# A fused sliding-window attention and feed-forward kernel: half-width PV matmuls in two batches, a reordered start, a split last tile

## The chip, the core and the metric

The kernel runs on one core of one Trainium2 chip. TensorE is called PE (its weight loads PEld), VectorE DVE, ScalarE ACT, GpSimd POOL and SyncE SP, as in the profile. The metric is the time of one launch on the device, in microseconds (us). Each engine works through its own instructions in program order, and semaphores order the engines among each other. DMAs are issued from the queues of SP and POOL, and after the change from ACT's as well.

## The reference

Eight batches of eight heads attend over 576 positions with head dimension 64. A query sees only itself and the 63 keys before it. The heads are joined to 512 columns, and a multiplicative feed-forward network follows.

```
def _attn_ref(q, k, v):              # 8 x 8 x 576 x 64, float32
    scores = scale * np.matmul(q, k.transpose(0, 1, 3, 2))
    rel = pos[:, None] - pos[None, :]
    scores = np.where((rel >= 0) & (rel < 64), scores, -1e9)
    attn = softmax(scores)
    return np.matmul(attn, v)

def _moe_ref(x, w1, w2, w3, w_out):  # x is 4608 x 512
    a = x @ w1                       # 512 -> 1024
    b = x @ w2
    h = a * b @ w3                   # 1024 -> 1024
    return h @ w_out                 # 1024 -> 512
```

## The kernel before, in words

**The weights are folded.** Since nothing nonlinear stands between them, w3 and w_out are multiplied once into one matrix `wc_sb`. `fold_t(fc)` transposes one of eight row blocks of w3 on PE (L446) and copies it out of PSUM on DVE (L448); `fold_mm(fc)` multiplies it with w_out on PE (L454, eight matmuls of 512 columns) and casts the result into `wc_sb` (L455). Two row blocks of w3 arrive with one DMA, `load_w3` (L439); w_out arrives whole with `load_wo` (L433). Both are cast to fp16 on the way, and so are v (`load_v`, L233) and w1 and w2 (`load_w12`, L429); all of these are issued from POOL.

**Attention** takes a batch in six units d of 192 queries by four heads (two head pairs jj, with heads a = 0 and 1 of each). q and k of a batch come from SP's queue (`load_qk`, L206), two DMAs each, one for each half hh of the heads. They are cast to fp16 (L221 in thirds for batch 0, L214 in halves later) and transposed on PE (L253) into PSUM tiles that DVE or ACT copies out (L257). For a unit, `scores(d)` makes the transposed scores (PE, L278), their exponential (ACT, L282) and the window mask with two or four selects (POOL, L290 and L292). `values(d)` is the product PV on PE (L311): eight matmuls, whose 128 weight columns are one head's 64 columns of v and 64 columns of ones, so that the output and the softmax sum of a head come out together, on the two halves of the partitions, for a = 0 and a = 1 the other way round. Then ACT takes the logarithm of the sums in two pieces of 64 partitions (L320, L321) and the exponential of its negative (L323), and DVE multiplies in two pieces of 64 partitions (L326, L327) into `xT`, the transposed input of the network. The tile `o_ps` of this product has one buffer, so the next unit's product waits for the last multiplication. The logarithms are also kept (`lnsum`, L332) for a range check at the end.

**The network** takes groups of 512 tokens: `ffn_ab(g, fc)` (PE L395; ACT copy L400; DVE product L401) and `ffn_o(g, t)` (PE L408; DVE copy L410), with the result stored from SP (L417).

**The order** is written out by hand for the first two batches: a start with dummy matmuls `keep_busy(n)` (L479) on PE between the waits, then batch 0's six values interleaved with the fold, then batch 1's with group 0 of the network. From there on a planner interleaves the units of batches 2 to 7 with the groups 1 to 8. At the start, POOL clears the ones columns of both v buffers (`ones_of`, L488), and then issues w_out, the first piece of w3, three blocks of v, three pieces of w3 and two more blocks of v. PSUM has eight banks: one for `tp`, two each for `s_ps` and `o_ps` (one tile each), and three tiles `f_ps` of one bank. `spare` hands out the two banks of an `s_ps` or `o_ps` tile for transposes.

Of the kernel before, what the change touches and what calls it, by code (L numbers as in the profile page):

```python
# [8 lines left out]
FP32 = mybir.dt.float32  # L9
FP16 = mybir.dt.float16  # L10
I32 = mybir.dt.int32
ALU = mybir.AluOpType
AF = mybir.ActivationFunctionType
PSUM = bass.MemoryType.PSUM

P = 128
# [128 lines left out]
def kernel(  # L145
# [11 lines left out]
    nc = tc.nc  # L157
    B, H, S, D = q.shape
    N = B * S
    DM = H * D  # L160
    DF = moe_w3.shape[0]
    scale = 1.0 / (D ** 0.5)
    NJ = H // 2
    TP, TI = 32, 18
    GT = 512
    NG = N // GT
    RING = 4 * S
    NU = 12 * B
    ND = 6 * B

    keep = ctx.enter_context(tc.tile_pool(name="keep", bufs=1))
    ident16 = keep.tile([P, P], FP16)
# [15 lines left out]
    dve_cp = nc.vector.tensor_copy  # L188
# [8 lines left out]

    raws, k16s, q16s = {}, {}, {}

    def load_qk(b, which, gate=None):  # L200
        src = k if which == "k" else q
        t = sb.tile([P, 2, TI * D], FP32, name="stage", bufs=4)
        if gate is not None:
            gate(t[:, 0, 0:1], 0.0)
        for hh in range(2):
            nc.sync.dma_start(out=t[:, hh], in_=src[b, hh:H:2].rearrange("j (p r) d -> p j (r d)", r=TI))  # L206
        raws[which, b] = t

    def cast_qk(b, which, hh, cp):
# [6 lines left out]
    def cast_third(b, which, c, cp):  # L216
        t = raws[which, b]
        if c == 0:
            (k16s if which == "k" else q16s)[b] = sb.tile([P, TI, P], FP16, name=which + "16", bufs=1)
        t16 = (k16s if which == "k" else q16s)[b]  # L220
        cp(t16[:, 6 * c:6 * c + 6].rearrange("p i (hh d) -> p hh i d", hh=2),  # L221
           t[:, :, 6 * c * D:6 * c * D + 6 * D].rearrange("p hh (i d) -> p hh i d", d=D))
# [4 lines left out]
    def load_v(b, *blocks):  # L227

        vh = v_heads(b)
        for c in blocks:  # L230
            lo = D if c == 4 else 0
            s0 = VBLK[c] + lo
            nc.gpsimd.dma_start(out=vh[lo:P, c], in_=v[b, :, s0:s0 + P - lo, :].rearrange("h s d -> s h d"))  # L233
# [10 lines left out]
    def transposes(b, which, *cs, into=None, cps=None):  # L244

        t16, dst = (k16s, kTs) if which == "k" else (q16s, qTs)
        if cs[0] == 0:
            dst[b] = sb.tile([P, NJ, S], FP16, name=which + "T")
        if into is None:
            into = [ps_t.tile([P, 6, P], FP16, name="tp")]  # L250
        for c, tp in zip(cs, into):
            for i in range(6):
                nc.tensor.transpose(tp[:, i, :], t16[b][:, 6 * c + i, :], ident16)  # L253
        if cps is None:
            cps = [dve_cp if which == "k" or c != 1 else act_cp for c in cs]
        for c, tp, cp in zip(cs, into, cps):
            cp(dst[b].rearrange("q j (p i) -> q j p i", i=TI)[:, :, :, 6 * c:6 * c + 6],  # L257
               tp.rearrange("q i (p j) -> q j p i", p=TP))
# [37 lines left out]
    def values(d):  # L296
        b, r = divmod(d, 6)
        si, jp = divmod(r, 2)
        j0 = 2 * jp
        v16 = v16s[b % 2]  # L300
        pt = probs.pop(d)
        seg = SEGS[si]
        q_base = seg[0][1]
        o_ps = ps_v.tile([P, 2, 512], FP32, name="o_ps")
        for jj in range(2):
            first = True
            for a in range(2):
                c0 = 0
                for bi, (k0, q0, n, _) in enumerate(seg):
                    o0 = a * 192 + q0 - q_base  # L310
                    nc.tensor.matmul(o_ps[:, jj, o0:o0 + n],  # L311
                                     v16[:, si * 2 + bi, j0 + jj, a * D:a * D + P],
                                     pt[:, a, jj, c0:c0 + n],
                                     start=first, stop=(bi == 1), skip_group_check=True)
                    first = False
                    c0 += n
        if jp == 0:
            lns[b, si] = sb.tile([P, NJ, 192], FP32, name="ln_s", bufs=4)
        y = lns[b, si][:, j0:j0 + 2]
        nc.scalar.activation(y[0:D], o_ps[D:P, :, 0:192], AF.Ln)  # L320
        nc.scalar.activation(y[D:P], o_ps[0:D, :, 192:384], AF.Ln)  # L321
        r = sb.tile([P, 2, 192], FP32, name="r")
        nc.scalar.activation(r, y, AF.Exp, scale=-1.0)  # L323
        x0 = (b * S + q_base) % RING
        xs = xT[:, j0:j0 + 2, x0:x0 + 192]
        nc.vector.tensor_tensor(xs[0:D], o_ps[0:D, :, 0:192], r[0:D], ALU.mult)  # L326
        nc.vector.tensor_tensor(xs[D:P], o_ps[D:P, :, 192:384], r[D:P], ALU.mult)  # L327

# [74 lines left out]

    def ffn_o(g, t):
        ab = abs_[g]
        o_ps = ps_f.tile([P, DM], FP32, name="f_ps")
        for fc in range(8):
            nc.tensor.matmul(o_ps, ab[:, fc, t * P:t * P + P], wc_sb[:, fc, :], start=(fc == 0), stop=(fc == 7))  # L408
        o_sb = sb.tile([P, DM], FP32, name="t2k", bufs=4)
        dve_cp(o_sb, o_ps)  # L410
        r0 = g * GT + t * P
        stores.append((r0, o_sb))

    def store():
        while stores:
            r0, o_sb = stores.pop()
            nc.sync.dma_start(out=out[r0:r0 + P, :], in_=o_sb)  # L417

    wo16 = sb.tile([P, 8, DM], FP16, name="ab", bufs=3)
    w3a = sb.tile([P, 8, DM], FP16, name="ab", bufs=3)  # L420
# [14 lines left out]
    def load_w3(n):  # L435
        fc = 2 * n
        dst = w3a[:, 2 * fc:2 * fc + 4, :].rearrange("p (f a) n -> p f (a n)", f=2) if n < 2 else \
            xT[:, fc - 4:fc - 2, 2 * S:2 * S + DF]
        nc.gpsimd.dma_start(out=dst, in_=moe_w3[fc * P:fc * P + 2 * P].rearrange("(f p) n -> p f n", p=P))  # L439

    def fold_t(fc):

        w3 = w3_rows(fc).rearrange("p a (e n) -> p (a e) n", n=P)
        tp = ps_f.tile([P, 8, P], FP16, name="f_ps")
        for ec in range(8):
            nc.tensor.transpose(tp[:, ec, :], w3[:, ec, :], ident16)  # L446
        w3T = sb.tile([P, 8, P], FP16, name="t2k", bufs=4)
        dve_cp(w3T, tp)  # L448
        return w3T

    def fold_mm(fc, w3T, cp):
        o_ps = ps_f.tile([P, DM], FP32, name="f_ps")
        for ec in range(8):
            nc.tensor.matmul(o_ps, w3T[:, ec, :], wo16[:, ec, :], start=(ec == 0), stop=(ec == 7))  # L454
        cp(wc_sb[:, fc, :], o_ps)  # L455
# [19 lines left out]
    def keep_busy(n):  # L475

        d = ps_t.tile([P, P], FP32, name="tp")
        for _ in range(n):
            nc.tensor.matmul(d, ident16, ident16, start=True, stop=True)  # L479


    load_qk(0, "k")
    load_qk(0, "q")
    nc.scalar.preload_act_table_set("natural_log_exp_and_others")
    make_identity(nc, ident16)

    def ones_of(i):
        nc.gpsimd.memset(v16s[i].rearrange("p c j (a e) -> p (c j a) e", a=2)[:, :, D:2 * D], 1.0)  # L488

    ones_of(0)  # L490
    ones_of(1)
    load_wo()
    load_w3(0)
    load_v(0, 0, 2, 3)
    for n in range(1, 4):
        load_w3(n)
    load_v(0, 4, 5)

    w3Ts = {}

    def fold_step(fc):
        if fc + 1 < 8:
            w3Ts[fc + 1] = fold_t(fc + 1)
        fold_mm(fc, w3Ts.pop(fc), act_cp if fc % 4 == 3 else dve_cp)

    def spare(pool, name):

        t = pool.tile([P, 2, 1024], FP16, name=name)
        return [t[:, i, 0:768].rearrange("p (i n) -> p i n", i=6) for i in range(2)]

    keep_busy(75)
    tps = spare(ps_s, "s_ps") + spare(ps_v, "o_ps")
    for c in range(3):
        cast_third(0, "k", c, act_cp if c == 1 else dve_cp)
    transposes(0, "k", 0, 1, 2, into=tps, cps=[dve_cp, act_cp, dve_cp])
    keep_busy(10)
    for c in range(3):
        cast_third(0, "q", c, act_cp if c == 1 else dve_cp)
    tps = [tps[3], ps_t.tile([P, 6, P], FP16, name="tp"), spare(ps_s, "s_ps")[0]]
    transposes(0, "q", 0, 1, 2, into=tps, cps=[act_cp, dve_cp, act_cp])  # L520
    keep_busy(15)
    scores(0)
    keep_busy(10)
    scores(1)
    keep_busy(30)
    for i in range(2):
        load_w12(i, 0)
    w3Ts[0] = fold_t(0)
    fold_step(0)
    fold_mm(1, w3Ts.pop(1), dve_cp)  # L530
    copy_v(0, 1)
    for d in range(5):
# [21 lines left out]
    cast_qk(1, "q", 1, act_cp)  # L554
    values(5)
    fold_step(7)
    transposes(1, "k", 0, 1, into=spare(ps_s, "s_ps"))
    transposes(1, "k", 2)
    for n in range(3):
        keep_sums(n)  # L560
    load_v(1, 5)
# [1 line left out]
    load_qk(2, "q")  # L563
    load_v(2, 0, 2, 3)
    ffn_ab(0, 0)
    transposes(1, "q", 0, 1, into=spare(ps_s, "s_ps"))
    transposes(1, "q", 2)
    copy_v(1, 1)


# [6 lines left out]
    for d in range(6, 11):  # L577
# [10 lines left out]
        else:  # L588
            which, hh = [("k", 0), ("k", 1), ("q", 0), ("q", 1)][d - 7]
            cast_qk(2, which, hh, pool_cp)  # L590
    transposes(2, "k", 0, 1, into=spare(ps_s, "s_ps"))
    values(11)
    transposes(2, "k", 2)
    for hh in range(2):
        cast_qk(3, "k", hh, pool_cp)
    ffn_o(0, 3)
    store()
    transposes(2, "q", 0, 1, into=spare(ps_s, "s_ps"))
    transposes(2, "q", 2)
    copy_v(2, 1)  # L600
    copy_v(2, 4)
    load_qk(3, "q")
# [68 lines left out]
```

## Time and profile before

| | us |
|---|---|
| median of 9 runs | 296.5 |
| lowest and highest of them | 296.13 and 297.53 |
| the profiled execution's own time | 297.87 |
| its span, first to last instruction | 295.9 |
| PE busy | 276.3 (93%) |
| POOL, DVE and ACT busy | 180.7, 185.5 and 168.4 |
| mean granted TensorE clock | 0.991 of full |

The profile shows one execution. A timeline row gives the start, the duration, the engine, the line, the operation, the tiles (out<-in), the form and the count of the instructions merged in it; in brackets stand the idle time before it and what ended that. A row of the chain of waits gives start, duration and what was under way; "issue" is time for which the profile shows no wait. A row of the windows gives the stretch, its length, the busy time of PE, PEld, DVE, ACT and POOL with instruction counts, the granted clock of TensorE, the mean busy share of the DMA engines (over 1 where packets overlap) and GB/s.

### The profile page before, as it was taken

Reading aid. Unit: us, or ns where it says so; the run is one execution under the profiler, and the core shown is the slowest. Engines: PE = TensorE matmul, PEld = TensorE weight load, DVE = VectorE, ACT = ScalarE, POOL = GpSimd, SP = SyncE. Lnnn points to the kernel's source line nnn. Section 1 sums busy time; section 2 is a strip of 40 time slices with the busy share of each in tenths; the row PEclk is TensorE's granted clock in tenths of the full one; section 3 lists DMA queues with packets and bytes.
Section 4 is the critical chain, followed back from the end, with each engine's and each line's share of the span. In section 5 each row is a group of like instructions: output and inputs, shape, how many; then the busy total and the mean of one; then the engine's idle time right before and its main releaser. Section 6 shows DMA issues by size and latency. Waiting matters only on the chain.

```text
span 295.9 us, 5925 instructions
## 1 busy us (share of the span) xinstructions
PE 276.3 (93%) x2254; PEld 154.5 (52%) x2254; DVE 185.5 (63%) x289; ACT 168.4 (57%) x281; POOL 180.7 (61%) x214
## 2 busy tenths in 40 slices
PE   7768998899889999999999999999999999999992
PEld 7654545444545555555555787555555444444440
DVE  0713688655796666778868766677868655554541
ACT  2421875586448638775686565497668866642300
POOL 8735897378839956597769453786595443402200
PEclk9998999999999999999999999999999999999998
DMA  6999999983267928295909380970095021012012
GB/s 235 211 181 201 262 275 200 364 134 52 73 209 309 80 93 287 88 65 134 336 19 112 120 309 2 116 112 1 3 160 66 0 74 72 0 38 108 0 59 92
DMA packets 51665, 38.85 MB, mean 131 GB/s; under 512 B 38784, under 2 KB 41856, under 8 KB 51632
## 3 DMA queue, kind: packets, MB, share of 16 engines
q0 software_dynamic: 41744, 9.96, 36.2%
q1 hardware_dynamic: 9888, 28.46, 26.5%
q8 instruction: 19, 0.31, 0.4%
q14 instruction: 14, 0.11, 0.1%
HBM read 38.80 MB, written 9.44 MB: 163 GB/s over the span
## 4 chain that ended last, share of the span: by engine, by line
PE 76%; DVE 6%; ACT 5%; DMA 4%; issue 3%; POOL 3%; POOLq 0%; DVEq 0%; ACTq 0%
PE f_ps L395 38%; PE f_ps L408 19%; PE o_ps L311 7%; PE tp L253 5%; DMA ab<-in_moe_w_dram 4%; PE s_ps L278 4%; PE f_ps L454 2%; DVE xT L327 2%; ACT ln_s L321 2%; ACT r L323 2%; POOL v L488 2%; DVE kT L257 1%; DVE xT L326 1%; ACT ln_s L320 1%; ACT pt L282 1%
## 5 line engine op out<-in xcount | busy, mean ns | idle before, releaser
L395 PE MATMUL f_ps<-xT,w_sb 128*128 128x512 f16 (+1 forms) x640 | 134.1, 358 | 0.0
L290 POOL TENSOR_SCALAR_AFFINE_SELECT pt<-pt 128x512 f16<-128x512 f16 (+1 forms) x64 | 52.1, 814 | 70.5 <-ACT pt L282 70.4
L395 PEld LDWEIGHTS <-w_sb 128*128 128x128 f16 x640 | 59.7, 98 | 50.8 <-issue 0.5
L408 PE MATMUL f_ps<-wc_sb,ab 128*128 128x512 f16 x288 | 67.1, 379 | 0.1
L401 DVE TENSOR_TENSOR ab<-f_ps,a_sb 128x512 f16<-128x512 f32 x72 | 49.8, 692 | 18.4 <-PE f_ps L395 15.7
L326 DVE TENSOR_TENSOR xT<-o_ps,r 64x384 f16<-64x384 f32 x48 | 26.4, 549 | 53.9 <-ACT r L323 52.4
L282 ACT ACTIVATE pt<-s_ps 128x1024 f16<-128x1024 f32 (+1 forms) x48 | 45.5, 949 | 18.2 <-PE s_ps L278 16.7
L400 ACT COPY a_sb<-f_ps 128x512 f32<-128x512 f32 x72 | 41.7, 579 | 24.8 <-PE f_ps L395 23.9
L292 POOL TENSOR_SCALAR_AFFINE_SELECT pt<-pt 128x512 f16<-128x512 f16 (+1 forms) x64 | 52.4, 819 | 4.4
L320 ACT ACTIVATE ln_s<-o_ps 64x384 f32<-64x384 f32 x48 | 23.4, 487 | 53.9 <-PE o_ps L311 53.8
L408 PEld LDWEIGHTS <-ab 128*128 128x128 f16 x288 | 26.9, 98 | 28.8 <-DVE ab L401 0.6
L233 POOL DMA_DIRECT2D v<-in_v_dram x40 | 33.9, 855 | 6.1 <-DMA ab<-in_moe_w_out_dram 4.3
L311 PE MATMUL o_ps<-pt,v 128*128 128x128 f16 (+1 forms) x384 | 27.9, 215 | 5.8 <-DVE xT L327 4.0
L311 PEld LDWEIGHTS <-v 128*128 128x128 f16 x384 | 23.6, 98 | 18.1 <-issue 4.7
L410 DVE COPY t2k<-f_ps 128x512 f32<-128x512 f32 x36 | 24.7, 690 | 11.6 <-PE f_ps L408 11.1
L327 DVE TENSOR_TENSOR xT<-o_ps,r 64x384 f16<-64x384 f32 x48 | 26.9, 561 | 0.7
L323 ACT ACTIVATE r<-ln_s 128x384 f32<-128x384 f32 x48 | 25.1, 522 | 1.5
L321 ACT ACTIVATE ln_s<-o_ps 64x384 f32<-64x384 f32 x48 | 23.1, 482 | 0.5
L278 PEld LDWEIGHTS <-kT 64*128 64x128 f16 x384 | 10.5, 94 | 16.4 <-issue 14.8
L278 PE MATMUL s_ps<-qT,kT 64*128 64x128 f16 (+1 forms) x384 | 18.2, 214 | 0.3 <-ACT pt L282 0.2
L454 PE MATMUL f_ps<-ab,t2k 128*128 128x512 f16 x64 | 16.6, 409 | 0.4 <-DVE t2k L448 0.3
L257 DVE COPY kT<-tp 128x768 f16<-128x768 f16 x17 | 16.2, 952 | 0.1
(59 smaller groups left out, 182.7 us busy)
## 6 DMA issues: line engine op xcount, KB each, us to landing
stage<-in_k_dram SPq DMA_DIRECT2D x16, 576.0 KB
stage<-in_q_dram SPq DMA_DIRECT2D x16, 576.0 KB
out_dram<-t2k SPq DMA_DIRECT2D x36, 256.0 KB
v<-in_v_dram POOLq DMA_DIRECT2D x32, 128.0 KB, 4.8
w_sb<-in_moe_w_dram POOLq DMA_DIRECT2D x4, 512.0 KB, 9.1
ab<-in_moe_w_out_dram POOLq DMA_DIRECT2D x1, 1024.0 KB, 10.6
ab<-in_moe_w_dram POOLq DMA_DIRECT2D x2, 512.0 KB, 12.8
xT<-in_moe_w_dram POOLq DMA_DIRECT2D x2, 512.0 KB, 16.4
```

What stands on the lines that cost most here:

```text
L233: nc.gpsimd.dma_start(out=vh[lo:P, c], in_=v[b, :, s0:s0 + P - lo, :].rearrange("h s d -> s h d"))
L278: nc.tensor.matmul(s_ps[:, a, jj, c0:c0 + n], kT[half, j, k0:k0 + P], qT[half, j, q0:q0 + n], start=True, stop=True, skip_group_check=True)
L282: nc.scalar.activation(pt[:, :, :, 0:w], s_ps[:, :, :, 0:w], AF.Exp, bias=-SHIFT, scale=scale)
L290: nc.gpsimd.affine_select(out=sl, in_=sl, pattern=pat, compare_op=ALU.is_ge, fill=0.0, base=off, channel_multiplier=-1)
L292: nc.gpsimd.affine_select(out=sl, in_=sl, pattern=[[-s, m] for s, m in pat], compare_op=ALU.is_ge, fill=0.0, base=63 - off, channel_multip ...
L311: nc.tensor.matmul(o_ps[:, jj, o0:o0 + n], v16[:, si * 2 + bi, j0 + jj, a * D:a * D + P], pt[:, a, jj, c0:c0 + n], start=first, stop=(bi = ...
L323: nc.scalar.activation(r, y, AF.Exp, scale=-1.0)
L327: nc.vector.tensor_tensor(xs[D:P], o_ps[D:P, :, 192:384], r[D:P], ALU.mult)
L395: nc.tensor.matmul(d[:, f * n + c0:f * n + c1], w[:, dc, (fc + f) * P:(fc + f + 1) * P], xT[:, dc, xc:xc + c1 - c0], start=first, stop=(dc ...
L400: act_cp(a_sb[:, 0:nf * n], a_ps[:, 0:nf * n])
L401: nc.vector.tensor_tensor(ab[:, fc:fc + nf, lo:hi], b_ps[:, 0:nf * n].rearrange("p (f n) -> p f n", f=nf), a_sb[:, 0:nf * n].rearrange("p ...
L408: nc.tensor.matmul(o_ps, ab[:, fc, t * P:t * P + P], wc_sb[:, fc, :], start=(fc == 0), stop=(fc == 7))
```

## The change

1. **PV in batches 0 and 1** (`SHORT = 2`). The eight matmuls with 128 weight columns become sixteen with 64: for every head, v alone and the ones alone. Head a writes the partitions a*64 to a*64+63, v into bank e = 0 of `o_ps` and the ones into bank e = 1. So both heads' outputs lie in one bank over all partitions and both sums in the other, and one logarithm, one exponential and one multiplication of 128 partitions do the unit. The other batches keep the old form.
2. **First loads.** `load_qk` takes a second queue; for batch 0 the half hh = 1 of k and of q is issued from ACT.
3. **POOL's order at the start.** The first piece of w3 goes ahead of w_out, and `ones_of(1)` goes behind the last block of v.
4. **PE's order at the start.** `fold_t(0)` and `fold_t(1)` move between and behind the first two scores; the dummy matmuls are 6, 4 and 45 in place of 15, 10 and 30. The casts and copies of q are dealt out differently between ACT and DVE.
5. **Banks of the transposes.** `spare` goes; `bank` hands out one bank of a tile, and `three()` takes one of `o_ps`, one of `tp` and one of `s_ps`. k of batch 0 uses the three `f_ps` tiles.
6. **The last output tile** is computed in two halves of 256 columns, one copied by ACT and stored from ACT's queue, the other copied by DVE and stored from SP's. `store()` takes from the front of its list.

```diff
-    def load_qk(b, which, gate=None):
+    def load_qk(b, which, gate=None, other=None):
...
-            nc.sync.dma_start(out=t[:, hh], in_=...)
+            (other if hh and other else nc.sync).dma_start(out=t[:, hh], in_=...)
...
     def values(d):
...
+        if b < SHORT:
+            for jj in range(2):
+                c0 = 0
+                for bi, (k0, q0, n, _) in enumerate(seg):
+                    o0 = jj * 192 + q0 - q_base
+                    for e in range(2):
+                        for a in range(2):
+                            nc.tensor.matmul(o_ps[a * D:a * D + D, e, o0:o0 + n],
+                                             v16[:, si * 2 + bi, j0 + jj, (2 * a + e) * D:(2 * a + e) * D + D],
+                                             pt[:, a, jj, c0:c0 + n],
+                                             start=(jj == 0 and bi == 0), stop=(bi == 1), skip_group_check=True)
+                    c0 += n
+            o, total = (o_ps[:, e, 0:384].rearrange("p (j n) -> p j n", j=2) for e in range(2))
+            nc.scalar.activation(y, total, AF.Ln)
+            nc.scalar.activation(r, y, AF.Exp, scale=-1.0)
+            nc.vector.tensor_tensor(xs, o, r, ALU.mult)
+            return
...
     def ffn_o(g, t):
...
+        halves = [(0, DM, dve_cp)] if (g, t) != (NG - 1, 3) else [(0, 256, act_cp), (256, DM, dve_cp)]
+        for c0, c1, cp in halves:
+            o_ps = ps_f.tile([P, DM], FP32, name="f_ps")
+            for fc in range(8):
+                nc.tensor.matmul(o_ps[:, 0:c1 - c0], ab[:, fc, t * P:t * P + P], wc_sb[:, fc, c0:c1], ...)
+            cp(o_sb[:, c0:c1], o_ps[:, 0:c1 - c0])
+            stores.append((r0, c0, c1, o_sb))
 
     def store():
         while stores:
-            r0, o_sb = stores.pop()
-            nc.sync.dma_start(out=out[r0:r0 + P, :], in_=o_sb)
+            r0, c0, c1, o_sb = stores.pop(0)
+            queue = nc.scalar if c1 - c0 < DM and c0 == 0 else nc.sync
+            queue.dma_start(out=out[r0:r0 + P, c0:c1], in_=o_sb[:, c0:c1])
...
-    load_qk(0, "k")
-    load_qk(0, "q")
+    load_qk(0, "k", other=nc.scalar)
+    load_qk(0, "q", other=nc.scalar)
...
     ones_of(0)
-    ones_of(1)
+    load_w3(0)
     load_wo()
-    load_w3(0)
     load_v(0, 0, 2, 3)
     for n in range(1, 4):
         load_w3(n)
     load_v(0, 4, 5)
+    ones_of(1)
...
+    def bank(pool, name):
+        t = pool.tile([P, 2, 1024] if name != "f_ps" else [P, 1, 1024], FP16, name=name)
+        return t[:, 0, 0:768].rearrange("p (i n) -> p i n", i=6)
+    def tp_bank():
+        return ps_t.tile([P, 6, P], FP16, name="tp")
+    def three():
+        return [bank(ps_v, "o_ps"), tp_bank(), bank(ps_s, "s_ps")]
 
     keep_busy(75)
...
-    transposes(0, "k", 0, 1, 2, into=tps, cps=[dve_cp, act_cp, dve_cp])
+    transposes(0, "k", 0, 1, 2, into=[bank(ps_f, "f_ps") for _ in range(3)], cps=[dve_cp, act_cp, dve_cp])
     keep_busy(10)
     for c in range(3):
-        cast_third(0, "q", c, act_cp if c == 1 else dve_cp)
+        cast_third(0, "q", c, dve_cp if c == 2 else act_cp)
...
-    keep_busy(15)
+    transposes(0, "q", 0, 1, 2, into=three(), cps=[act_cp, dve_cp, act_cp])
+    keep_busy(6)
     scores(0)
-    keep_busy(10)
+    keep_busy(4)
+    w3Ts[0] = fold_t(0)
     scores(1)
-    keep_busy(30)
+    w3Ts[1] = fold_t(1)
+    keep_busy(45)
     for i in range(2):
         load_w12(i, 0)
-    w3Ts[0] = fold_t(0)
-    fold_step(0)
+    fold_mm(0, w3Ts.pop(0), dve_cp)
     fold_mm(1, w3Ts.pop(1), dve_cp)
...
-    transposes(1, "k", 0, 1, into=spare(ps_s, "s_ps"))
-    transposes(1, "k", 2)
+    transposes(1, "k", 0, 1, 2, into=three())
...
-    transposes(2, "k", 0, 1, into=spare(ps_s, "s_ps"))
+    transposes(2, "k", 0, 1, into=[bank(ps_s, "s_ps"), tp_bank()])
     values(11)
     transposes(2, "k", 2)
...
-    transposes(2, "q", 0, 1, into=spare(ps_s, "s_ps"))
-    transposes(2, "q", 2)
+    transposes(2, "q", 0, 1, 2, into=three())
```

q of batch 1 is changed as k of batch 1 is.

## The prediction

> **What bounds the kernel now.** I read the windows first, to see where PE is not full, then the timeline of those stretches, then the chain of waits, then the last rows. Two windows:
>
> ```profile
> 20.00:40.00 20.00, 17.94 (x163) 9.87 (x161) 10.75 (x20) 9.14 (x16) 15.41 (x20) 0.91 1.29 246
> ...
> 100.00:120.00 20.00, 20.00 (x161) 10.50 (x160) 13.88 (x24) 11.75 (x20) 13.59 (x17) 1.00 0.65 181
> ```
>
> From about 91 us to 290 us PE is busy all the time, in code that the change leaves alone but for its last tile. A shift won before 91 us therefore reaches the end whole, and nothing else does but the tail. Before 91 us PE waits, and at 20 to 40 us it also has a clock of only 0.91. The timeline tells why:
>
> ```profile
> 16.03 1.85 PE L479 MATMUL tp<-ident 128*128 128x128 f16 x30
> ...
> 17.46 0.70 POOL L233 DMA_DIRECT2D v<-in_v_dram  x1 [4.25 <-DMA ab<-in_moe_w_out_dram]
> ...
> 19.75 1.07 PE L446 MATMUL f_ps<-ident,ab 128*128 128x128 f16 x16 [1.87 <-DMA ab<-in_moe_w_dram]
> ...
> 21.15 5.20 PE L454 MATMUL f_ps<-ab,t2k 128*128 128x512 f16 x16 [0.34 <-DVE t2k L448]
> ```
>
> PE idles from 17.88 to 19.75 for the first piece of w3. The clock then drops (0.58 in the window 20.4 to 23.8), and the sixteen fold matmuls take 5.20 us; at the 0.216 us apart that L454 shows later they would take 3.46. The first values, behind them, run at 27.78. From there the chain of waits repeats every 3.4 to 3.5 us:
>
> ```profile
> 37.97 0.62 PE o_ps L311 x8
> 38.64 0.47 issue
> 39.11 0.49 ACT ln_s L321
> 39.62 0.53 ACT r L323
> 40.22 0.53 issue
> 40.74 0.57 DVE xT L327
> 41.36 0.64 PE o_ps L311 x8
> ```
>
> The reader should see a ring: product, two logarithms (the first hides under "issue"), exponential, two multiplications, next product. In such a period PE issues 3.05 us of work and stands 0.43 us. In batch 1 the same wait costs PE, by its waits from 59 to 91 us:
>
> ```profile
> PE o_ps L311 <- DVE xT L327: 1.9, 3, 0.7
> PE tp L253 <- DVE kT L257: 1.2, 1, 1.2
> ```
>
> The end:
>
> ```profile
> 290.05 0.69 DVE L410 COPY t2k<-f_ps 128x512 f32<-128x512 f32 x1 [1.03 <-PE f_ps L408]
> ```
>
> SP issues the last store at 290.77, the trace's semaphore records have it landed at 293.93, and 1.97 us of closing steps follow.
>
> [...] the last L311 and the first L278 matmul, which uses half the rows, start 0.152 us apart where the spacing is 0.055, so a switch costs 0.10. [...] This trace has only row halves: L278 starts in pairs 3 ns apart, a pair every 0.055 us. [...] the four first loads land at 5.56, 6.97, 8.57 and 10.01, 590 KB every 1.4 to 1.6 us, some 410 GB/s.
>
> **The change, part by part.** The times are of the profiled execution.
>
> *PV, on PE.* 12 units have 16 weight loads and matmuls in place of 8. If the a = 0 and a = 1 matmuls pair as L278's do, eight pairs stream as many columns as eight matmuls did: 0.44 us for 128 columns each. The mode switch on entering adds 0.10, uneven pairing and slower weight loads say 0.05: **+0.15 a unit**, which I take. It can't be below 0. Without pairing it is 16 x 0.055 + 0.10 - 0.44 = +0.54; with a whole weight load (98 ns in L311's row) exposed each time 16 x 0.098 + 0.10 - 0.44 = +1.23. The range takes the first two; the last is a rival.
>
> *PV, the ring.* One logarithm (0.49) and one multiplication (0.56) go. L320 takes 0.487 on 64 partitions and L323 0.522 on 128 with as many elements a partition, so the remaining ones keep their length. The ring falls from 3.48 to about 2.6 and no longer binds; PE's 3.05 + 0.15 does, or POOL.
>
> *POOL at the start.* `ones_of(1)` takes 2.66 us (L488) and leaves the front, so every DMA of this queue is issued 2.66 us sooner, the first w3 piece at 4.05 in place of 7.72. It shares the engines with q until about 9.5; I count w3 landed at 12 and w_out (5.1 us of data at the 205 GB/s that the packets reach later) at 18.0, where w_out and w3 together took until 19.70. Behind w_out stand three blocks of v and the other w3 pieces as before; they move with it, the second piece to about 22.2 (24.76 before), just ahead of `fold_t(2)`. ACT issues two loads (about 0.6 each) ahead of its table load (1.28): done by 3.5, hidden under the wait for k. k's earlier landing gains little, because `keep_busy(75)` holds PE until 8.46.
>
> *PE at the start.* Separate banks let ACT copy kT without waiting for DVE (2.43 before), ACT takes two thirds of q's casts as its copies end (q still lands at 10.0, so little moves), and nine dummies fewer let `scores(0)` go at 13.9 (14.50 before). `fold_t(0)`, `scores(1)` and `fold_t(1)` fill PE to 16.2, 45 dummies of 0.056 to 18.7. Then w_out is there, the clock is full, and `fold_mm(0)` and `(1)` end at 22.3 (before 26.4). With the cast (0.69) and the two copies of v (0.6) the first values come at 23.75. POOL: the last v block waits for w_out (18.0), takes 0.9, then comes the moved memset to 21.55 and four selects (2.1) to 23.7, level with PE. **-4.0 here**; if w_out lands 1.5 us later, everything moves with it and -2.5 remains.
>
> *Batch 0.* POOL's selects and DMA issues now follow without a gap and end unit 5 at 40.3 (PE's values(5) at 44.86 before). What is late next is the DMA of batch 1's q: issued 12.3 us before its landing at 44.62, and ACT's cast of it began at 44.65, ahead of unit 5's logarithm. Issued 4.1 sooner, beside w1 and w2 that are now still moving, I have it land at 40.8; cast 1.15, logarithm at 42.1, where 45.82 was: -3.7. The transposes of k now wait for unit 5's multiplication, since they use its bank: **-3.6 on leaving batch 0**.
>
> *Banks later.* The 0.4 us that PE waits at 50.5 for s_ps goes: **-0.4**. At 77 to 83 us the stall of 1.2 only moves: the third kT transpose now waits for the copy of the second out of tp, where the third of q did. 0, within 0.3.
>
> *Batch 1.* 1.9 us of waits go, 6 x 0.15 of PE come, and POOL (selects 2.25 and a cast 1.14 a unit, 3.4) lets only half of the rest through: **-0.5**.
>
> *Tail.* The last copy is 256 columns, about 0.42 in place of 0.69, and the last DMA half as long (0.3); two more semaphores cost 0.1: **-0.4**. The half matmuls (L395's 256-column ones, 0.109 apart) cost nothing more. ACT is idle there. The order of `store()` changes nothing, as one tile at a time is pending.
>
> Sum: -3.6 - 0.4 + 0 - 0.5 - 0.4 = **-4.9**. On 297.87 that is 293.0; the median of the runs shown is 1.37 lower, so **291.6**.
>
> **The rivals.**
> 1. *PV in single file, weight loads hidden* (+0.54 a unit). For: no column pair in the trace. Against: the row pairs. Batch 1 turns from -0.5 to +1.3, batch 0 loses about 0.5: -2.6, **293.9**.
> 2. *DMA binds the start.* w_out lands at 19.5, as its slow beginning (102 and 127 KB a us at 9 to 11 us) may recur: -1.5 less, **293.1**; with q of batch 1 late too, 294.5.
> 3. *Nothing binds behind the start*: q in time, POOL faster because DVE does less: -7, **289.5**.
> 4. *Slower: exposed weight loads.* PE becomes the bound of both batches: of some 8.2 us to win with a free PV, PE's growth eats 11 units' worth, so the sign turns at +0.75 a unit, a mean spacing of 69 ns for the sixteen matmuls. At 98 ns (+1.23) the kernel loses 5.3: **301.8**. [...]
> 5. *The change is not what it says*: the pairs would not be next to each other. They are in PE's program, 104 matmuls more.
>
> **How the numbers follow.** A measurement here can tell about 0.2% (0.6 us) from no change. Forecast (289.9 to 292.9) 0.52, rival 1 0.14, rival 2 0.13, rival 3 0.08, rival 4 0.10, and 0.03 for cancelling effects between. Slower: rival 4 and a little of 1 and 2, 0.12; same 0.05; faster 0.83. The range 289.4 to 295.3 takes in rivals 1 to 3 and leaves rival 4 out.
>
> **What would show it.** After: no wait of PE for w3 near 20 us and clock 1.00 there; L454's first sixteen in 3.5 us; first values near 23.8; sixteen PV matmuls in pairs, 0.5 us a unit; one logarithm and one multiplication; ACT's cast of q waiting for its DMA near 41; PE full from about 87; last landing 3 us before the end. PV spaced over 69 ns, or first values after 26 us, would make it wrong.

## The result, and the profile after

The changed kernel takes **292.22 us** (median of 10 runs, 290.9 to 293.27) where the kernel before takes 296.44 (31 runs). The ratio is 0.9849, with a 95% interval from 0.9832 to 0.9865. The forecast was 291.6 with a range of 289.4 to 295.3. The total was right, but the experiments show that its parts were not: the start was put too high, the gain from the short PV too low, and the banks had the wrong sign.

The profiled execution after took 291.12 us, with a span of 289.2. That is 6.7 less than the span before, more than the medians' 4.2, because the profiled execution before lay 1.4 above its median and this one lies 1.1 below its own.

First the two windows that were shown of before, now of after:

```profile
20.00:40.00 20.00, 18.42 (x211) 10.49 (x210) 13.62 (x22) 10.35 (x16) 19.44 (x24) 1.00 1.22 257
100.00:120.00 20.00, 20.00 (x162) 10.39 (x160) 14.52 (x23) 12.74 (x23) 11.62 (x16) 1.00 0.48 171
```

From 20 to 40 us the clock is full (1.00, before 0.91), and POOL has become the busiest engine, with 19.44 us of 20 (15.41 before). At 100 us PE is as full as before.

The timeline of the start:

```profile
16.20 2.68 PE L503 MATMUL tp<-ident 128*128 128x128 f16 x45
...
18.71 3.62 PE L478 MATMUL f_ps<-ab,t2k 128*128 128x512 f16 x16
18.99 2.68 POOL L512 MEMSET v<- 128x3072 f16 x1
...
23.31 0.62 PE L470 MATMUL f_ps<-ident,ab 128*128 128x128 f16 x8 [0.98 <-DMA ab<-in_moe_w_dram]
23.86 0.58 PE L320 MATMUL o_ps<-pt,v 128*64 128x128 f16 x16
```

The wait for w3's first piece is gone, the fold's sixteen matmuls take 3.62 us in place of 5.20, and the first PV runs at 23.86 in place of 27.78. A new wait of 0.98 us for w3's second piece stands just ahead of it. The end of batch 0:

```profile
41.10 0.64 PE L320 MATMUL o_ps<-pt,v 128*64 128x128 f16 x16 [1.18 <-POOL pt L293]
41.49 1.15 ACT L215 CAST q<-stage 128x1152 f16<-128x1152 f32 x1 [1.72 <-DMA stage<-in_q_dram]
...
42.55 0.48 ACT L326 ACTIVATE ln_s<-o_ps 128x384 f32<-128x384 f32 x1
...
44.24 0.50 PE L254 MATMUL o_ps<-ident,k 128*128 128x128 f16 x6 [0.67 <-ACT wc_sb L479]
```

PE waits for POOL's select; ACT's only logarithm of unit 5 stands behind the cast of batch 1's q, which waited for its DMA; and the transposes of k come after that. In batch 1 one stall of PE remains:

```profile
74.14 0.50 PE L254 MATMUL tp<-ident,k 128*128 128x128 f16 x6 [1.27 <-DVE kT L258]
```

The shares of the chain of waits, which no longer has much of DVE and ACT (6% and 5% before):

```profile
PE 77%; DMA 11%; POOL 4%; DVE 2%; ACT 1%; issue 1%; SPq 1%; POOLq 0%; ACTq 0%
```

### The profile page after: what moved, and what is told of

Same layout as the page of the kernel before. It is cut to its first block, busy times and chain, and to the rows that moved or that the text cites. A ratio compares the mean times of both kernels' runs of the same rounds, so it can differ in the third digit from the quotient of the medians.

```text
span 289.2 us, 6101 instructions
## 1 busy us (share of the span) xinstructions
PE 274.6 (95%) x2358; PEld 155.3 (54%) x2358; DVE 179.7 (62%) x276; ACT 164.2 (57%) x271; POOL 180.9 (63%) x214
## 4 chain that ended last, share of the span: by engine, by line
PE 77%; DMA 11%; POOL 4%; DVE 2%; ACT 1%; issue 1%; SPq 1%; POOLq 0%; ACTq 0%
PE f_ps L414 39%; PE f_ps L432 22%; DMA stage<-in_q_dram 6%; DMA ab<-in_moe_w_dram 5%; PE o_ps L336 5%; PE tp L254 5%; PE s_ps L279 4%; PE o_ps L320 1%; POOL v L234 1%; POOL v L512 1%; SPq L207 1%; POOL pt L293 1%; POOL pt L291 1%; DVE t2k L434 1%; PE f_ps L478 1%
## 5 line engine op out<-in xcount | busy, mean ns | idle before, releaser
L432 PE MATMUL f_ps<-wc_sb,ab 128*128 128x512 f16 (+1 forms) x296 | 67.0, 373 | 0.1
L345 DVE TENSOR_TENSOR xT<-o_ps,r 64x384 f16<-64x384 f32 x36 | 19.8, 550 | 39.6 <-ACT r L344 39.6
L432 PEld LDWEIGHTS <-ab 128*128 128x128 f16 x296 | 27.6, 98 | 27.9 <-issue 0.3
L342 ACT ACTIVATE ln_s<-o_ps 64x384 f32<-64x384 f32 x36 | 17.6, 488 | 32.6 <-PE o_ps L336 32.6
L434 DVE COPY t2k<-f_ps 128x512 f32<-128x512 f32 (+1 forms) x36 | 24.5, 683 | 13.2 <-PE f_ps L432 12.7
L336 PEld LDWEIGHTS <-v 128*128 128x128 f16 x288 | 18.1, 98 | 8.7 <-ACT pt L283 0.8
L336 PE MATMUL o_ps<-pt,v 128*128 128x128 f16 (+1 forms) x288 | 20.7, 215 | 0.4 <-POOL pt L293 0.4
L346 DVE TENSOR_TENSOR xT<-o_ps,r 64x384 f16<-64x384 f32 x36 | 20.2, 560 | 0.5
L344 ACT ACTIVATE r<-ln_s 128x384 f32<-128x384 f32 x36 | 18.9, 525 | 1.2
L343 ACT ACTIVATE ln_s<-o_ps 64x384 f32<-64x384 f32 x36 | 17.4, 483 | 0.4
L258 DVE COPY kT<-tp 128x768 f16<-128x768 f16 x18 | 17.1, 952 | 0.2
L326 ACT ACTIVATE ln_s<-o_ps 128x384 f32<-128x384 f32 x12 | 5.9, 491 | 18.5 <-PE o_ps L320 18.5
```

The costliest lines, as they stand in the source:

```text
L336: nc.tensor.matmul(o_ps[:, jj, o0:o0 + n], v16[:, si * 2 + bi, j0 + jj, a * D:a * D + P], pt[:, a, jj, c0:c0 + n], start=first, stop=(bi = ...
L432: nc.tensor.matmul(o_ps[:, 0:c1 - c0], ab[:, fc, t * P:t * P + P], wc_sb[:, fc, c0:c1], start=(fc == 0), stop=(fc == 7))
L434: cp(o_sb[:, c0:c1], o_ps[:, 0:c1 - c0])
```

## The experiments

Each kernel ran in five rounds beside the kernel before, so each has a ratio to it. The difference of a kernel to the changed kernel is that of the two ratios times 296.4 us; its interval is the root of the sum of squares of the two half-widths. The table puts five profiles side by side (times in us from the span's start; for before, after and three experiments that are told below).

| | before | e1: change without short PV | e2: short PV alone | after | f1: five edits on top |
|---|---|---|---|---|---|
| first PV of batch 0 goes through | 27.78 | 23.80 | 26.32 | 23.86 | 21.59 |
| PV of unit 5 | 44.86 | 41.32 | 42.43 | 41.10 | 39.67 |
| scores(6) | 55.17 | 54.94 | 52.23 | 51.52 | 49.47 |
| scores(12) | 84.81 | 86.68 | 78.57 | 79.03 | 75.82 |
| span | 295.9 | 297.0 | 289.7 | 289.2 | 286.0 |
| ratio of times to before | 1 | 1.002 | 0.9819 | 0.9849 | 0.975 |

### PV: taken out, alone, in one batch, in all

**e1_old_pv** is the change with the old PV.

```diff
-    SHORT = 2
+    SHORT = 0
```

> The changed kernel with SHORT = 0: the new start, banks and tail, but PV as before in all batches. Theory (the short PV gives batch 0 only one logarithm and one multiplication behind its last unit, about 1.0 us, because POOL and q's landing hold the rest, and batch 1 about 2.1): first values still near 23.9, 292.2 + 3.1 = 295.3 us. Rival (the shorter ring carries batch 0 too, 0.4 us a unit): 297.3 us. Rival (the start carries nearly all, as the prediction's sum has it with 0.5 for batch 1): 293.5 us.

Measured: **297.81 us**, ratio 1.002 (1.000 to 1.0041), which is 297.0 against the 296.4 of before. The rival with the full ring gain (297.3) is the nearest; the other two expectations were too low. Without the short PV the other five parts bring nothing, or lose; the short PV is worth 5.1 ± 0.8 us in the change. The table says where the start's lead goes: 4.0 us at the first PV, 3.5 at unit 5, 0.2 at scores(6), and a loss of 1.9 at scores(12). The timeline of e1 shows it:

```profile
46.00 0.73 PE L254 MATMUL o_ps<-ident,k 128*128 128x128 f16 x6 [2.14 <-DVE xT L346]
...
47.80 2.75 PE L414 MATMUL f_ps<-xT,w_sb 128*128 128x512 f16 x8
...
80.12 0.72 PE L254 MATMUL tp<-ident,k 128*128 128x128 f16 x6 [1.75 <-DVE kT L258]
80.63 3.39 PE L432 MATMUL f_ps<-wc_sb,ab 128*128 128x512 f16 x8
```

k's transposes now need the bank of `o_ps`, and wait 2.14 us for the second multiplication of the old PV. (Before, they ran in `s_ps` while that multiplication was still due.) At the second place the third block of k waits for the copy out of `tp`. After both waits TensorE's clock is down: eight matmuls of 512 columns take 2.75 and 3.39 us where they take 1.89 elsewhere, and the mean granted clock is 0.89 in the windows 45 to 60 and 75 to 90 us, 1.00 in the one between. So the long PV and the new banks hurt each other. No kernel ran with the old PV, the new start and the old banks, so how much of the start's lead the old PV alone would have left is not known.

**e2_only_pv** is the kernel before with the new block of `values` and nothing else.

```diff
+        if b < SHORT:      # SHORT = 2, sixteen matmuls, one logarithm, one exponential, one multiplication
...
+            return
```

> The kernel before with the short PV in batches 0 and 1 and nothing else. Theory: values(0) stays at 27.8, q of batch 1 still lands near 44.6 and holds the last logarithm of batch 0, so batch 0 gives about 1.0 us and batch 1 about 2.1: 296.4 - 3.1 = 293.3 us. Rival (behind an unchanged start q's landing eats all of batch 0, and batch 1 is worth the predicted 0.5): 295.7 us.

Measured: **291.39 us**, ratio 0.9819 (0.9794 to 0.9844), better than every expectation. One part of the change gives at least what the whole gives (the whole is 0.9 ± 0.9 us behind it). By the table e2 gains on before 1.0 from the first PV to unit 5, 0.5 from there to scores(6) and 3.3 from scores(6) to scores(12). The last has two parts: the six units (from the start of batch 1's first PV to that of its last 18.0 us, 20.1 before), and the stall of 1.17 us of the third q block for the copy of kT, which is gone. DVE has one multiplication a unit less and makes its copies in time. The remaining 1.5 us, ahead of the first PV, are not the edit's: POOL's and PE's orders are those of before, and w3 arrives as late (PE takes up the fold at 19.65, before at 19.75). But the clock stays up (1.00 in every window of 2 us from 18 to 28):

```profile
19.65 1.07 PE L465 MATMUL f_ps<-ident,ab 128*128 128x128 f16 x16 [0.51 <-DMA ab<-in_moe_w_dram]
21.05 3.63 PE L473 MATMUL f_ps<-ab,t2k 128*128 128x512 f16 x16 [0.34 <-DVE t2k L467]
...
26.32 0.43 PE L320 MATMUL o_ps<-pt,v 128*64 128x64 f16 x12 [0.69 <-DVE v L240]
```

In this execution the half-speed stretch fell on the dummies and first scores, from 14 to 17 us (0.50 in the window 14 to 16, 0.71 in 16 to 18), and the fold took 3.63 us and not 5.20.

**e5_short1**: batch 1 with the old PV (`SHORT = 1`).

> The changed kernel with SHORT = 1: batch 1's PV as before. Theory (batch 1 is worth what the two traces show, values(6) to scores(12) 2.1 us shorter): 294.3 us. Rival (the predicted term, 0.5; the traces differ by something else): 292.7 us.

Measured: 295.11 us, ratio 0.9937 (0.9919 to 0.9955): batch 1 is worth 2.6 ± 0.7 us. The theory (2.1) holds, the prediction's 0.5 does not. The stall for kT at 77 us is 1.75 us here, as in e1, against 1.27 in the changed kernel.

**e9_short8**: the short PV in all batches (`SHORT = 8`).

> The changed kernel with the short PV in all eight batches, where PE is the bound. Theory (from the distance between the first PV and the first score matmul, 0.570 us against 0.539): 36 units at +0.03, 293.3 us or less where ring waits went. Rival (the prediction's +0.15 a unit): 297.6 us. Rival (column halves in single file, +0.54): over 310 us.

Measured: **299.10 us**, ratio 1.0104 (1.0085 to 1.0123), 7.6 ± 0.7 us slower than the change. Over 36 units, where PE is the bound, that is **0.21 us a unit**: the prediction's 0.15 was the better guess, the theory (0.03) fell. It had looked only at the side of the scores, and their first matmul starts 0.152 us behind the last of the old PV (before, at 34.9 us) as behind the last of the new (the changed kernel, at 30.5). Between two FFN products both sides show, first in the changed kernel (old PV there), then in e9:

```profile
130.53 1.89 PE L432 MATMUL f_ps<-wc_sb,ab 128*128 128x512 f16 x8
132.26 0.61 PE L336 MATMUL o_ps<-pt,v 128*128 128x128 f16 x8
132.71 1.89 PE L414 MATMUL f_ps<-xT,w_sb 128*128 128x512 f16 x8
```

```profile
133.23 1.89 PE L432 MATMUL f_ps<-wc_sb,ab 128*128 128x512 f16 x8
135.05 0.64 PE L320 MATMUL o_ps<-pt,v 128*64 128x128 f16 x16
135.62 1.90 PE L414 MATMUL f_ps<-xT,w_sb 128*128 128x512 f16 x8
```

From the FFN's start to PV's start 1.73 against 1.82, from PV's start to the next product 0.45 against 0.57: 0.09 us ahead of the short PV, and 0.12 from its start on. Within PV the heads a = 0 and a = 1 start in pairs, 3 to 4 ns apart. The second pair follows the first after 0.08 us and the others follow every 0.055 to 0.056, as the old matmuls did, so the pairs add 0.03. From the last start to the next product it is 0.15 in place of 0.06, so the step to the next product costs 0.10. In these runs the short PV thus pays in batches 0 and 1, where a ring of ACT and DVE is the bound (5.1 us in the change), and costs 0.21 us a unit in batches 2 to 7, where PE is.

### The start

**e3_pool_order**: POOL's order of before at the start.

```diff
     ones_of(0)
-    load_w3(0)
+    ones_of(1)
     load_wo()
+    load_w3(0)
...
-    ones_of(1)
```

> The changed kernel with POOL's order of before at the start: both memsets of v first, then w_out, then w3's first piece. Theory (the order of POOL's queue is what brings the first values forward): w3 and w_out land together near 19.7, PE stands before the fold and its clock drops, first values near 26.4; q of batch 1 follows, so the 2.5 us go through to the end: 294.7 us. Rival (with the memset out of the way POOL no longer holds batch 0, and half of the loss is made up): 293.4 us.

Measured: 295.33 us, ratio 0.9952 (0.9933 to 0.9972), 3.1 ± 0.8 us slower than the change. The theory's sign and size hold, but the place was worse than it said: `fold_t(0)` now stands ahead of scores(1) in PE's order, so PE waited 5.67 us for w3 until 19.58, the clock was half from 18.2 to 25.0 (0.54, 0.50, 0.50 and 0.75 in the windows of 2 us from 18 to 26), and the first PV went through at 30.88. PE's new order needs POOL's; in this form the two are one edit.

**f3_sp_loads**: all four first loads on SP's queue.

```diff
-    load_qk(0, "k", other=nc.scalar)
-    load_qk(0, "q", other=nc.scalar)
+    load_qk(0, "k")
+    load_qk(0, "q")
```

> The changed kernel with the first four loads all on SP's queue. Theory (k lands some 0.45 us later, but w_out at 17.8 sets the start of the fold): no change, 292.2 us. Rival (the second queue's 0.45 us go through to the fold): 292.7 us.

Measured: 291.59 us, ratio 0.9827 (0.9802 to 0.9852), 0.7 ± 0.9 faster than the change. The second queue brings nothing that can be measured, as the theory had it.

**f2_fold_behind**: the transposes that wait for w3's second piece go behind the first PV.

```diff
-        if d == 0:
-            w3Ts[2] = fold_t(2)
         values(d)
         if d < 4:
             scores(d + 2)
+        if d == 0:
+            w3Ts[2] = fold_t(2)
```

> The changed kernel with fold_t(2) behind values(0) and scores(2), nothing else. Theory (w3's second piece, which landed between 23.3 and 24.6 in the runs so far, holds the first values, and the longer waits cost clock as well): 291.0 us. Rival (POOL's memset and first selects, done at 23.8, hold the first values just as late): 292.2 us.

Measured: 291.98 us, ratio 0.9839 (0.9812 to 0.9867), 0.3 ± 1.0 from the change: the number is the rival's, the mechanism is neither's. The first four matmuls of PV start at 22.94, as soon as POOL's select is done, and the other twelve then wait for DVE:

```profile
22.94 0.30 PE L320 MATMUL o_ps<-pt,v 128*64 128x128 f16 x4 [0.18 <-POOL pt L293]
23.52 0.36 DVE L238 COPY v<-v 64x512 f16<-64x512 f16 x1
23.91 0.60 DVE L240 COPY v<-v 64x512 f16<-64x512 f16 x1
...
24.57 0.43 PE L320 MATMUL o_ps<-pt,v 128*64 128x64 f16 x12 [1.33 <-DVE v L240]
```

The copies of v stand on DVE behind the casts of the two fold products. So v's copies were what came late next.

### Banks, q, memset

**e4_old_banks**: the transposes of batches 1 and 2 on the banks of before.

```diff
-    transposes(1, "k", 0, 1, 2, into=three())
+    transposes(1, "k", 0, 1, into=spare(ps_s, "s_ps"))
+    transposes(1, "k", 2)
...             # the same for q of batch 1, k and q of batch 2
```

> The changed kernel with the transposes of batches 1 and 2 on the banks of before (two tiles in s_ps, the third in tp); batch 0's stay on the new ones. Theory (the new banks set k's transposes of batch 1 behind the last multiplication of batch 0, 1.0 us and 0.67 of waiting, and stall the third kT transpose at 74 us for 1.27; PE idle for so long also loses clock in some executions): both waits go, the 0.4 us wait for s_ps in batch 1 comes back: 290.5 us. Rival (the prediction's step: the banks gain 0.4 and the stall only moves): 292.6 us.

Measured: **290.13 us**, ratio 0.9787 (0.977 to 0.9804), 1.8 ± 0.7 us faster than the change. The theory's number holds, and one half of its mechanism. From scores(6) to scores(12) its profile takes 26.35 us, the changed kernel's 27.51: the stall of 1.27 us at 74 us is gone, and the third block of k does not wait:

```profile
73.83 0.51 PE L254 MATMUL tp<-ident,k 128*128 128x128 f16 x6
```

The other half does not show: from unit 5's PV to scores(6) e4 takes 10.90 us and the changed kernel 10.42, for in place of the wait of 0.67 stand one of 0.52 for unit 5's multiplication and one of 0.37 for a copy of kT. So 1.2 of the 1.8 us are found in the traces, and the rest is not.

Beside e2, which has the short PV alone, e4 tells what the start, batch 0's new banks and the tail add to it: 0.9 ± 0.9 us. Its first PV starts at 24.75, 1.6 ahead of e2's 26.32, but scores(6) comes at 52.55 and scores(12) at 78.90 (e2: 52.23 and 78.57). In this execution the start's lead was gone before scores(6). The timeline of e4 shows what the start still costs in some executions, and the windows the clock there:

```profile
24.20 0.62 PE L470 MATMUL f_ps<-ident,ab 128*128 128x128 f16 x8 [2.54 <-DMA ab<-in_moe_w_dram]
...
25.93 1.03 PE L470 MATMUL f_ps<-ident,ab 128*128 128x128 f16 x8
26.76 2.69 PE L478 MATMUL f_ps<-ab,t2k 128*128 128x512 f16 x8
```

```profile
24.00:26.00 2.00, 1.80 (x33) 1.44 (x34) 0.69 (x1) 0.49 (x1) 1.86 (x5) 0.74 1.11 209
26.00:28.00 2.00, 2.00 (x12) 1.21 (x12) 1.16 (x2) 1.44 (x2) 2.00 (x4) 0.50 1.49 187
28.00:30.00 2.00, 2.00 (x28) 1.03 (x28) 0.52 (x1) 0.04 (x1) 1.93 (x3) 0.91 1.66 187
```

PE waits 2.54 us for w3's second piece, then the clock is half for a while (0.50 in the window 26 to 28). The clock falls short of full by 0.26, 0.50 and 0.09 in three windows of 2 us, which makes 0.85 x 2 / 0.5 = 3.4 us at half speed.

**e6_q_behind**: unit 5's values are written ahead of ACT's cast of batch 1's q.

```diff
-    cast_qk(1, "q", 1, act_cp)
     values(5)
+    cast_qk(1, "q", 1, act_cp)
```

> The changed kernel with values(5) written ahead of ACT's cast of batch 1's q, so that unit 5's logarithm no longer stands behind that DMA. Theory (q's landing is what is late next, with POOL's last select close behind it): the logarithm goes at about 41.7 in place of 42.55 and all behind moves: 291.4 us. Rival (q's landing is the only thing in the way, POOL's waits are slack): 290.3 us. Rival (the cast then delays wc_sb's copy, which k's transposes waited for): 292.2 us.

Measured: 290.86 us, ratio 0.9841 (0.9818 to 0.9865), 0.2 ± 0.9 from the change. This does not tell the expectations apart. Its profile waits 2.7 us for w3's second piece, like e4's.

**e8_three**: e4's and e6's edits, and the second memset on VectorE at the start.

```diff
-        nc.gpsimd.memset(
+        (nc.vector if i else nc.gpsimd).memset(
...
     ones_of(0)
+    ones_of(1)
...
-    ones_of(1)
```

> The changed kernel with three edits: the old banks for the transposes of batches 1 and 2, values(5) ahead of q's cast, and the second memset of v's ones on VectorE at the very start, where it idles, in place of POOL's 2.7 us at 19 us. Theory (POOL's 1.7 us of waits in batch 0 and q's landing hide each other, so that only together they give their time): values(5) near 39.7, the first FFN product of batch 0 near 42.7 in place of 45.2, the stall at 74 us gone: 288.2 us. Rival (first pieces of w1 and w2, or v of batch 1, come late instead): 290 us.

Measured: 289.96 us, ratio 0.9783 (0.9766 to 0.9801): not to be told from e4 (290.13). The theory fell in this run (f1 below comes to the times it put), and the rival's 290 came without its reason. POOL's waits in batch 0 are gone from the profile and unit 5 to scores(6) takes 9.80 us (10.90 in e4), but its start is later: PE waited 2.7 us for w3 and the first PV ran at half clock (0.65 and 0.50 in the windows from 24 and 26 us): from 25.53, and 0.85 us long where f1's first PV takes 0.54.

### The tail, and all together

**f4_whole_tile**: the last tile whole, from DVE and SP.

```diff
-        halves = [(0, DM, dve_cp)] if (g, t) != (NG - 1, 3) else [(0, 256, act_cp), (256, DM, dve_cp)]
+        halves = [(0, DM, dve_cp)] if True else [(0, 256, act_cp), (256, DM, dve_cp)]
```

> The changed kernel with the last output tile whole, copied by VectorE and stored by SP. Theory (the prediction's tail, 0.4): 292.6 us. Rival (the tails of the two traces, 4.45 against 5.13 us from the last store's issue to the end, 0.7): 292.9 us.

Measured: 292.90 us, ratio 0.9867 (0.9839 to 0.9895), 0.5 ± 1.0 slower than the change. The medians are where both expectations have them, but the interval also holds zero. The traces show the copy, first of the changed kernel, then of f4:

```profile
283.83 0.36 ACTq L441 DMA_DIRECT2D out_dram<-t2k  x1
284.30 0.42 DVE L434 COPY t2k<-f_ps 128x256 f32<-128x256 f32 x1 [1.05 <-PE f_ps L432]
```

```profile
285.75 0.69 DVE L434 COPY t2k<-f_ps 128x512 f32<-128x512 f32 x1 [1.03 <-PE f_ps L432]
```

From the start of this copy to the end of the span it is 4.9 us in the changed kernel (289.2 - 284.30) and 5.75 in f4 (291.5 - 285.75). The other profiles say the same: from 4.3 to 5.0 us in all eleven with the split tile, 5.8 to 5.9 in the three with the whole one (before, e2, f4). The split therefore gains about 1 us by the traces, where the run times alone leave it open.

**f1_five**: e8 with f2's edit and v's copy between the two first fold products.

```diff
     fold_mm(0, w3Ts.pop(0), dve_cp)
+    copy_v(0, 1)
     fold_mm(1, w3Ts.pop(1), dve_cp)
-    copy_v(0, 1)
```

> The kernel with three edits (old banks for batches 1 and 2, values(5) ahead of q's cast, VectorE's memset) and two more: fold_t(2), which waits for w3's second piece, goes behind values(0) and scores(2), and v's copy goes between the two first fold products. Theory (in the run with three edits PE stood 2.7 us before fold_t(2) and its clock fell, 1.03 us for eight transposes in place of 0.62): 0.9 us of other work fills the wait, what is left is short enough for the clock to stay, and some 2 us come off: 287.8 us. Rival (the transfers set the pace, w3's pieces, then k, q and v of batch 1): 289.5 us.

Measured: **288.77 us**, ratio 0.975 (0.9716 to 0.9785), 2.9 ± 1.1 us faster than the changed kernel: the best of all versions. The last two edits are worth 1.0 ± 1.1 over e8, between the two expectations and not settled by these runs. Its clock (the page's row of 40 slices) and its timeline:

```profile
PEclk9999999999999999999999999999999999999998
```

```profile
21.59 0.54 PE L320 MATMUL o_ps<-pt,v 128*64 128x128 f16 x16
...
24.16 1.07 PE L470 MATMUL f_ps<-ident,ab 128*128 128x128 f16 x16 [1.70 <-DMA ab<-in_moe_w_dram]
...
42.98 1.89 PE L414 MATMUL f_ps<-xT,w_sb 128*128 128x512 f16 x8
```

The first PV follows the fold at once. The wait for w3 is shorter, since PV and scores(2) lie in it, and no clock is lost there in this execution (1.00 in every window of 2 us from 8 to 36). (Two of f1's six runs had a mean clock of 0.985 and 0.982 and took 289.73 and 291.1 us.) The first FFN product of batch 0 starts at 42.98, in the changed kernel at 45.24.

## Why the prediction was right in total, and where its steps failed

- **POOL's order and the fold: right in place, half right in cause.** The fold was to run from 18.7 to 22.3 and the first values at 23.75; the trace has 18.71 to 22.33 and 23.86. The place was in part luck: the changed kernel's profile has half clock from 11.79 to 15.20, and in e1, e4 and f1, at full clock there (1.00), the dummies end sooner and the fold starts at 18.03 to 18.05. And the step took the whole difference to before's profile, 4.0 us, for the change's. e2 has the old start and its first PV at 26.32, since the half-speed stretch lay elsewhere in that execution (14 to 17 us). So about 2.5 of the 3.9 us are the change's own. Where the half clock fell varied between the executions, as the last section shows. I had read before's one profile as if the clock always fell there.
- **w3's second piece** was to land at 22.2, "just ahead" of its reader, and no wait was put for it. It landed at 23.26, and PE waited 0.98 us; in e4, e6 and e8 it waited 2.5 to 2.7.
- **Batch 0: right in the times, in part wrong in the cause.** POOL is what follows (waits of 0.53 and 1.18), then q's landing, at 41.47 where 40.8 was put. The first FFN product came 3.0 sooner and scores(6) 3.65, for 3.6 and 4.0 predicted. But e2, with the old start, has scores(6) only 0.7 later (1.5 us of its lead, ahead of the first PV, came with the clock), and e1, with the new start, has nearly all of its lead gone by then. What the start won got through batch 0 only with the short PV.
- **Banks: the sign failed.** The step had a gain of 0.4 for s_ps and "0, within 0.3" for the stall that moves. e4 says that the new banks cost 1.8 ± 0.7. The gain is there (the wait is back in e4, with 0.37), but the stall would not have moved but gone: in e2 and e4, with the old banks, no wait of PE for kT is left between 70 and 80 us. The likely reason is that the short PV takes one multiplication a unit off DVE, which makes those copies.
- **Batch 1: mis-sized.** -0.5 was put, on the ground that POOL would let only half through and PE would take 0.9. The traces show -2.1, and e5 2.6 ± 0.7. POOL held only the first unit, twice, for 0.8 us in all.
- **PV on PE: right for these batches.** That column halves start in pairs was an estimate from the row pairs of the scores; they came so, 3 to 4 ns apart. +0.15 a unit was put. By the traces it is about 0.12 where scores follow (0.09 ahead of PV, and 0.570 in place of 0.539 us from the first PV to the first score matmul), and 0.21 in e9, where a full-width product follows 0.15 us behind PV's last matmul in place of 0.06, which the step left out.
- **Tail: too small.** -0.4 was put. The traces say about -1, and f4's 0.5 ± 1.0 does not speak against it. The 0.1 for two semaphores was the author's estimate; a semaphore instruction takes 17 ns on SP in before's trace and 51 on PE in the changed kernel's.

In the sum, the start and the banks were credited with what the short PV gives. By e1 the change without it is no faster than the kernel before, and by e2 it alone gives 5.4 ± 0.7 us. The prediction's only term for it alone was the 0.5 of batch 1; in batch 0 it was a part of the 3.6. The errors had opposite signs and cancelled, so that the right total was luck. A shift at 91 us did reach the end whole, as the prediction had it: e2 leads by 6.2 us at scores(12) and by 6.2 at the end. But a lead won at 24 us did not reach 91: in e1 it was used up by the waits behind it.

## What to carry to other kernels

Ask of a lead won early which wait behind it will take it back, and test each part of a change alone and left out: a right total can hide two wrong terms. A shorter ring can also take load off the engine that makes other copies (in e2 the stall of 1.17 us for kT went), so count the stalls that vanish with it. Before a gain is read from one profile, look whether a clock drop in that execution makes up part of it (of the 3.9 us at the first PV some 1.5); and look at PE's idle times close together as well as each for itself: e1's half clock at 80 us came behind waits of 0.48 and 1.75 us, 2.4 us apart.

## What the runs showed of the hardware

- **Half speed came in stretches of 3.41 us.** Before's trace has a clock of 0.50 from 20.97 to 24.38 us, the changed kernel's from 11.79 to 15.20, and 1.00 on both sides of it. By windows of 2 us from 8 to 36 us, eight profiles have one such stretch, three (e3, e5, f3) one of 6.8, f4 two of 3.4, e1 and f1 none there; the clock in it is 0.50. Its place varied between executions: from 12 us in the changed kernel's profile, from 21 in before's, from 25 in e4's. In the three executions with two stretches apart, their starts lie 34.14 us apart in e1 (46.10 and 80.24), 13.66 in f4 (11.66 and 25.32) and 64.86 in e5 (12.41 and 77.27), which is ten, four and nineteen times 3.41 to 3.42.
- **How much idle time went ahead of it.** All 14 profiles were cut into pieces of 3.41 us from 6 to 280 us, in step with their half-speed stretches (f1's with the place where its dummy matmuls change from half to full speed, at 6.76 us). Each of the 16 pieces at full clock in which PE idled 1.84 us or more was followed by one at half clock, and none of those with 1.70 or less. A half-speed piece went over into a second one with 0.64 us of idle time or more (e3, e5, f3), and ended with 0.41 or less. One wait of 1.75 us (e1, at 78 us, with 0.48 of idle time just ahead of it in the same piece) was followed by half speed, and f1's wait of 1.70 was not: a border at 23.83 parts it into 1.37 and 0.33. This is what these profiles show; they have no piece between 1.70 and 1.84 at full clock, nor between 0.41 and 0.64 at half.
- **What a stretch cost.** By its length and clock (3.41 us at 0.50) it takes 1.7 us of PE's work, an estimate that e1's second stretch bears out: six transposes took 0.72 us where they take 0.50 elsewhere, and the eight matmuls behind them 3.39 where they take 1.89. It cost less over dummy matmuls that fill a wait anyway: the fold started at 18.71 in the changed kernel's profile, at 18.04 in e4's, where the dummies ran at full clock (1.00).
- **The two column halves of the short PV ran side by side, in pairs.** In e9 sixteen matmuls with 64 weight columns take 0.42 us from the first start to the last, eight with 128 columns 0.39 in the changed kernel. Their weight loads take 110 ns each, a little more than the 98 of the full width; sixteen of them lie in 0.48 us of e9's timeline, under the matmuls. The price beside FFN products was 0.09 us ahead of the first matmul (0.309 us behind the last FFN matmul in place of 0.216 in the changed kernel's trace), 0.10 behind the last and 0.03 at the first pair.
